# A planner's priorities replaced by a fixed table of task order, and second-layer expert weights loaded into batch tiles as these come free

## The chip, the cores and the metric

The kernel runs on one core of a Trainium2 chip. The metric is device time in microseconds (us), the median of the runs shown. The core has a matrix engine (TensorE, PE), a vector engine (VectorE, DVE), a scalar engine (ScalarE, ACT), a general engine (GpSimd, POOL) and a queue engine that here only issues transfers (SyncE, SP). POOL and ACT can issue transfers (DMAs) too. Each engine takes its instructions in the order of the program, and waits at an instruction until what it needs is there.

## The reference

For 8 batches of 3072 tokens and 256 channels the kernel computes a Fourier mixing layer, a soft mixture of experts over all tokens, and a gated feed-forward layer:

```python
X = np.fft.rfft(x, axis=1)
Yr = Xr @ w_r - Xi @ w_i + b_r
Yi = Xr @ w_i + Xi @ w_r + b_i
Yr = np.sign(Yr) * np.maximum(np.abs(Yr) - lam, 0.0)
Yi = np.sign(Yi) * np.maximum(np.abs(Yi) - lam, 0.0)
y = np.fft.irfft(Y, n=x.shape[1], axis=1)
...
logits = x @ phi
d = np.exp(logits - logits.max(0)); d /= d.sum(0) + 1e-09
slot_input = d.T @ x
h = np.maximum(slot_input[e] @ w1[e], 0.0)
slot_out[e] = h @ w2[e]
c = np.exp(logits - logits.max(1)); c /= c.sum(1) + 1e-09
x = c @ slot_out
...
g = x @ w_gate
silu = g * (1.0 / (1.0 + np.exp(-g)))
val = x @ w_val
return (silu * val @ w_out).astype(np.float32)
```

The second softmax (`d`) runs over all 24576 tokens, so no expert can start before the last batch is through.

## The kernel before

There are three parts. **The planned part** treats the eight batches. The transform of 3072 points is split into 96 x 32: `stage_a` (PE, then a transposition `turn` on DVE) makes the 96-point half from quarters of `x` (`load_x`, two buffers), `stage_c` the 32-point half for three groups of frequencies, with evacuations on ACT and DVE, `stage_b` multiplies by the mixed weights (bank `pb`), `after_b` applies the threshold (`take`, `gather`, two `relu`, and `join`, a subtraction). `stage_q` multiplies the result `yt` by `phi` (PE products that are 32 columns wide, four side by side), turns `yt` on DVE (`turn_y`) and copies it in 16 pieces to the slots' layout `yi` with DMAs (`spread`). When three groups are through, `logits` goes back to the time domain (`inv_mm` from `qt`), takes maxima and exponentials, `slots` transforms these forward again (`rot` and `cross` are its rotations, `d_mm` a product) and multiplies them by `yi` (`slot_mm`, again 32 wide; `acc` gathers over the batches), `combine` prepares the third softmax and stores it. In between, `narrow` converts the weights of the last layer, which arrive as 64-bit numbers, in 18 pieces: load, `bits` and `value` on DVE, `size` on ACT, store.

Every step is a task that names what it reads, writes and needs. `Plan` holds them; rings (`plan.ring`) say how many buffers a kind of tile has. `Plan.run` is a list scheduler: it holds a model of each engine with durations (`COST`), a rank for each task with a correction (`SHIFT`), and always emits the task that can start first. So all engines' orders come out of this one loop. A task for `POOL` or `DVE` goes where the model has it done sooner. `hold` is a filler for PE: a product of the identity that nobody reads, taken only when PE would be idle.

**The expert part** (`after_slots`) needs `acc` from all batches. `stage1` multiplies by the first-layer weights (`w1s`, 1 MB for each of 8 experts), `turn` transposes, `stage2` multiplies by the second-layer weights (`w2s`, 1 MB each), in two rounds of four experts. First-layer loads are issued by POOL from the seventh batch on. Of the second-layer loads one goes out on POOL into a `yi` buffer; the other seven are issued by SP, when the last batch's `yi` pieces are through and the pool `bpool` (the batches' tiles) is closed by `free_b`, into a new pool `w2p` in its place. After them SP loads the gate weights (`fetch_wg`, three tiles `wg`).

**The steady part** first makes the gates (`gates`, tile `pq`), then runs 576 steps `gv`, `split`, `mm_out` over all tokens; its order is written out and not the planner's.

The key of the scheduler, in `Plan.run`, is:

```python
                    start = max(free.get(eng, 0.0) + turn, can, lock if pair(t, eng) else 0.0)
                    late = self.SHY if eng == "DVE" and len(t["eng"]) > 1 else 0.0
                    key = (start + late + self.PULL * t["rank"], t["rank"], start + late + dur, i)
```

Of the kernel before, what the change touches and what calls it, by code (L numbers as in the profile page):

```python
# [176 lines left out]
SHIFT = {  # L177
    "load_f": 57.75,
    "setup_small": -9.60,
    "load_first": -50.92,  # L180
    "stage_a.mm": -37.34,
    "stage_a.turn": 178.17,
    "put": 21.58,
    "free_early": -22.55,
    "load_w": 17.51,
    "mix_w": 61.49,
    "part_w": 18.49,
    "rest_w": -44.08,
    "stage_c.mm": (-53.77, 60.00, -28.03),
    "stage_c.hi": (67.58, -4.36, -34.90),  # L190
    "stage_c.lo": (-43.26, 302.18, -37.48),
    "stage_c.one_part": (-45.81, -35.81, 101.37),
    "stage_c.add_part": (-86.88, 268.31, 3.85),
    "stage_c.sum_hi": (-10.55, -273.23, -22.13),
    "stage_c.sum_lo": (-20.53, 76.87, -19.92),
    "stage_c.last_mm": (77.17, -43.48, -22.30),
    "stage_c.last_out": (64.11, 2.06, 26.30),
    "stage_b.last_mm": (-36.93, 87.21, 10.64),
    "stage_b.last_out": (61.99, -49.29, 73.95),
    "stage_b.mm": (59.64, 39.68, 49.11),  # L200
    "after_b.take": (184.64, -139.65, -117.21),
    "after_b.gather": (160.13, -11.80, -62.89),
    "after_b.relu": (577.81, 16.03, 90.14),
    "after_b.join": (15.07, 342.92, 39.20),
    "stage_q.mm": (77.93, -329.29, -32.38),
    "stage_q.turn_y": (0.20, 193.63, -56.74),
    "stage_q.turn": (130.59, 74.27, 57.66),
    "stage_q.spread": (11.96, 122.22, 36.67),
    "logits.inv_mm": 8.02,
    "logits.sp_mm": 56.11,  # L210
    "logits.sp_out": -28.82,
    "logits.rot": 154.63,
    "logits.join": 49.80,
    "logits.turn": -29.07,
    "logits.l_mm": 8.04,
    "logits.colmax": 29.69,
    "logits.keep_l": 48.70,
    "logits.spread": 152.32,
    "logits.max_mm": -95.72,
    "logits.newmax": 11.02,  # L220
    "logits.factor": -30.34,
    "logits.bc_mm": -17.70,
    "logits.lower": 61.38,
    "logits.expo": 71.85,
    "slots.f_mm": -192.46,
    "slots.turn": 242.98,
    "slots.cross": 121.42,
    "slots.rot": -1492.94,
    "slots.join": 46.30,
    "slots.d_mm": -85.36,  # L230
    "slots.evac": -50.96,
    "slots.slot_mm": -0.37,
    "slots.gather": -37.26,
    "combine.rowmax": 980.32,
    "combine.lower": -94.57,
    "combine.expo": 30.36,
    "combine.total": 0.43,
    "combine.scale": -18.67,
    "combine.turn": 30.84,
    "combine.hi": 77.39,  # L240
    "combine.lo": 100.87,
    "combine.store": 99.47,
    "narrow.load": -15.44,
    "narrow.bits": 876.30,
    "narrow.size": -12.04,
    "narrow.value": -46.30,
    "narrow.store": -30.91,
    "load_x": 70.05,
    "narrow.part": -34.22,
    "narrow.rest": 42.69,  # L250
    "stage_q.mm'": (33.76, 59.91, 56.58),
    "stage_q.turn_y'": (15.84, 57.75, 66.51),
    "stage_q.turn'": (-73.17, -38.23, -63.13),
    "stage_q.spread'": (-79.12, -25.52, 3.84),
    "logits.inv_mm'": -43.32,
    "logits.sp_mm'": 58.71,
    "logits.sp_out'": 7.77,
    "logits.rot'": 26.85,
    "logits.join'": 98.80,
    "logits.turn'": 6.52,  # L260
    "logits.l_mm'": 27.21,
    "logits.colmax'": 31.11,
    "logits.keep_l'": 106.81,
    "logits.spread'": -3.41,
    "logits.max_mm'": -5.61,
    "logits.newmax'": 3.65,
    "logits.factor'": 8.54,
    "logits.bc_mm'": 107.77,
    "logits.lower'": -53.83,
    "logits.expo'": 10.94,  # L270
    "slots.f_mm'": 44.65,
    "slots.turn'": 29.30,
    "slots.cross'": 150.69,
    "slots.rot'": -35.92,
    "slots.join'": 40.15,
    "slots.d_mm'": 40.12,
    "slots.evac'": -10.89,
    "slots.slot_mm'": -39.73,
    "slots.gather'": -26.36,
    "combine.rowmax'": -21.56,  # L280
    "combine.lower'": -6.29,
    "combine.expo'": 33.50,
    "combine.total'": -63.42,
    "combine.scale'": -88.17,
    "combine.turn'": -137.59,
    "combine.hi'": 68.96,
    "combine.lo'": -28.54,
    "combine.store'": 69.48,
    "free_x": -87.13,
    "free_a": -92.66,  # L290
    "free_b": 58.33,
    "fetch_w1": 102.65,
    "fetch_w2": 19.16,
    "fetch_wg": 51.16,
    "hold": 519.95,
    "stage_c.mm'": 31.70,
    "stage_c.hi'": 180.69,
    "stage_c.lo'": 40.92,
    "stage_c.one_part'": -78.25,
    "stage_c.add_part'": 37.03,  # L300
    "stage_c.sum_hi'": 68.22,
    "stage_c.sum_lo'": 8.91,
    "stage_b.mm'": 107.80,
    "after_b.take'": -12.15,
    "after_b.gather'": -45.62,
    "after_b.relu'": -8.39,
    "after_b.join'": 21.85,
# [1616 lines left out]
```

## Time and profile before

| | |
|---|---|
| median of 3 runs | 1716.13 us (1716.11 to 1717.84) |
| the profiled execution | 1717.98 us |
| its span (first to last instruction) | 1716.2 us |
| mean granted clock of PE | 0.997 |
| PE busy | 1676.7 us (98%), 8176 matrix instructions |
| DVE busy | 1276.8 us (74%) |
| ACT busy | 983.0 us (57%) |
| POOL busy | 351.3 us (20%) |
| DMA | 139.95 MB, mean 82 GB/s |
| longest groups on PE | `mm_out` with `hh` 722.5 us, with `hl` 453.8 us |

The planned part ends near 600 us, the steady loop begins near 640. An engine's busy share says little here: PE is the bound nearly everywhere, and what it loses is seen in its waits and in the time that its instructions take. A matrix instruction in a row of the timeline is an entry; several entries make a product.

### The profile page before, as it was taken

The numbers are of one execution on the slowest core, as the hardware profiler recorded it, in microseconds if no ns is written. First come the engines' busy times: TensorE is split into PE (matmuls) and PEld (weight loads), VectorE is DVE, ScalarE is ACT, GpSimd is POOL, SyncE is SP. The second block draws the span as 40 slices with busy tenths as digits, with TensorE's granted clock in tenths as the row PEclk, the third lists the DMA queues.
The fourth block names the chain that finished last, engine by engine and source line by source line (L and its number), as shares of the span: only waits on it lengthen the run. The fifth ranks groups of instructions, "written<-read, shape, count | busy, mean of one in ns | idle before, by whom it ended". The sixth has DMA issues, their size and how long they took to land.

```text
span 1716.2 us, 23315 instructions
## 1 busy us (share of the span) xinstructions
PE 1676.7 (98%) x8176; PEld 1283.8 (75%) x8176; DVE 1276.8 (74%) x2156; ACT 983.0 (57%) x1830; POOL 351.3 (20%) x392
## 2 busy tenths in 40 slices
PE   7999999999999979999999999999999999999998
PEld 4677676776767638888888888888888888888886
DVE  4677878878786628777777777777777877877776
ACT  2565554655556326666655656666666655666664
POOL 1345433344444620200200100010110110110000
PEclk9999999999999999999999999999999999999999
...
GB/s 188 80 105 149 113 136 132 111 157 112 144 141 137 236 337 14 81 25 25 78 28 26 49 57 25 29 72 18 25 81 25 25 80 25 25 71 25 25 25 25
DMA packets 260421, 139.95 MB, mean 82 GB/s; under 512 B 210224, under 2 KB 244240, under 8 KB 260304
## 3 DMA queue, kind: packets, MB, share of 16 engines
...
q14 instruction: 52, 0.43, 0.1%
...
## 4 chain that ended last, share of the span: by engine, by line
PE 89%; DMA 3%; DVE 3%; ACT 2%; SPq 2%; issue 1%; POOL 0%; ACTq 0%; DVEq 0%
PE o L1804 47%; PE pb L881 10%; PE pg L1779 8%; PE pv L1780 8%; PE ac L764 6%; PE ac L786 4%; PE ch L1050 1%; PE ch L979 1%; SPq L1008 1%; PE ch L1252 1%; DMA wg<-w_scr 1%; DVE xg L808 1%; PE ch L1304 1%; DMA w2s<-in_moe_w_dram 1%; DVE sf L814 1%; DMA cvi<-in_moe_w_out_dram 1%
## 5 line engine op out<-in xcount | busy, mean ns | idle before, releaser
L1804 PE MATMUL o<-hh,wo 128*128 128x512 f32 x2304 | 722.5, 394 | 0.0
L1782 ACT ACTIVATE sg<-pg 128x512 f32<-128x512 f32 x576 | 344.9, 599 | 418.0 <-PE pg L1779 418.0
L1784 DVE TENSOR_TENSOR h<-sg,pv 128x512 f32<-128x512 f32 x576 | 393.5, 683 | 251.2 <-ACT sg L1782 248.8
L1804 PEld LDWEIGHTS o<-hh,wo 128*128 128x128 f32 x2304 | 434.3, 188 | 100.8
L1804 PE MATMUL o<-hl,wo 128*128 128x512 f32 x1152 | 453.8, 394 | 0.0
L1792 DVE TENSOR_TENSOR hl<-h,hh 128x512 fp32r<-128x512 f32 x576 | 398.0, 691 | 0.1
L1791 ACT ACTIVATE hh<-h 128x512 fp32r<-128x512 f32 x576 | 359.3, 624 | 0.2 <-DVE h L1784 0.2
L1804 PEld LDWEIGHTS o<-hl,wo 128*128 128x128 f32 x1152 | 216.1, 188 | 51.8
L1779 PE MATMUL pg<-cst,gstk 96*128 96x512 f32 x576 | 227.8, 395 | 0.0
L1780 PE MATMUL pv<-cst,gstk 96*128 96x512 f32 x576 | 226.0, 392 | 0.0
L953 POOL TENSOR_TENSOR yt<-r,yt 128x512 f32<-128x512 f32 x96 | 125.5, 1307 | 166.8 <-ACT yt L944 91.8
L881 PE MATMUL pb<-xg,wh 128*128 128x512 f32 x384 | 142.5, 452 | 2.0 <-ACT yt L934 1.6
L1780 PEld LDWEIGHTS pv<-cst,gstk 96*128 96x128 f32 x576 | 109.7, 190 | 25.1
L1779 PEld LDWEIGHTS pg<-cst,gstk 96*128 96x128 f32 x576 | 108.1, 188 | 25.7 <-DVE gstk L1765 0.8
L1840 POOL TENSOR_TENSOR e<-e,rs 96x256 f32<-96x256 f32 x28 | 22.2, 818 | 500.0 <-DVE rs L1837 500.0
L769 DVE STREAM_TRANSPOSE chan<-ac 128x512 f32<-128x512 f32 x128 | 89.3, 706 | 36.6 <-PE ac L764 33.5
L764 PE MATMUL ac<-xq,fwd 96*128 96x512 f32 x224 | 110.2, 603 | 1.7 <-DVE m L1130 1.1
L786 PEld LDWEIGHTS ac<-cm,chan 128*128 128x128 f32 x768 | 99.3, 196 | 14.0 <-issue 7.0
L786 PE MATMUL ac<-cm,chan 128*128 128x128 f32 x768 | 104.8, 285 | 0.8 <-ACT sg L823 0.8
L881 PEld LDWEIGHTS pb<-xg,wh 128*128 128x128 f32 x384 | 66.9, 189 | 34.9 <-issue 19.6
L827 POOL TENSOR_TENSOR sg<-sf,sg 128x256 fp32r<-128x256 f32 x96 | 69.9, 741 | 88.9 <-ACT sg L823 72.7
L814 DVE TENSOR_TENSOR sf<-ac,sf 128x256 f32<-128x256 f32 x96 | 40.4, 421 | 49.9 <-ACT sf L811 21.2
...
## 6 DMA issues: line engine op xcount, KB each, us to landing
out_dram<-ob SPq DMA_DIRECT2D x190, 128.0 KB, 2.8
...
w2s<-in_moe_w_dram SPq DMA_DIRECT2D x7, 1024.0 KB, 12.9
x<-in_x_dram SPq DMA_DIRECT2D x4, 768.0 KB, 11.6
...
```

The lines of the kernel that those rows point to most:

```text
L764: nc.tensor.matmul(out=pt, lhsT=fwd[:, 8 - 8 * dh:136 - 8 * dh], rhs=T[kq][:, :, d1:d1 + 16], start=True, stop=True)
L769: nc.vector.transpose(out=chan[:, 12 * dh:12 * dh + 16, d0:d0 + 16, :].rearrange("p j d i -> p d j i"), in_=T[ka].rearrange("p n d -> p d n"),
L786: nc.tensor.matmul(out=pt[:, :, q:q + 2, i // 2, :], lhsT=chan[:, 16 * dh + j // 2, :, j % 2], rhs=cm[:, j, :].rearrange("p (c h k) -> p c ...
L881: nc.tensor.matmul(out=pt, lhsT=w[:, dh, m, es], rhs=xx, start=m != 1 and dh == 0 and n == 0, stop=dh == 1 and n == 2, skip_group_check=True,)
L953: e.tensor_sub(out=part(), in0=quarters(T[kr]), in1=part())
L1779: nc.tensor.matmul(out=pg, lhsT=gstk[:, 0, f * 128:(f + 1) * 128], rhs=rhs, start=True, stop=True)
L1780: nc.tensor.matmul(out=pv, lhsT=gstk[:, 1, f * 128:(f + 1) * 128], rhs=rhs, start=True, stop=True)
L1782: nc.scalar.activation(out=sg, in_=pg, func=AF.Silu)
L1784: nc.vector.tensor_mul(out=h, in0=sg, in1=pv)
L1791: nc.scalar.activation(out=hh, in_=h, func=AF.Copy)
L1792: nc.vector.tensor_sub(out=hl, in0=h, in1=hh.bitcast(F32))
L1804: nc.tensor.matmul(out=po_t[0][k], lhsT=w[:, f % 4, k * 128:(k + 1) * 128], rhs=a, start=(f == 0 and m == 0), stop=(f == NF - 1 and m == 2 ...
```

## The change

The tables `SHIFT`, `COST` and `PAIR` and the scheduler go. In their place stands `ORDER`, a table of task numbers; a negative number means that the task goes to the second of its two engines (DVE). `Plan.run` only emits the tasks in this order, and stops if one comes before what it needs. Each task keeps its work. Besides the order:

- The second-layer loads all go out on POOL, into tiles of the batches: experts 0 to 3 into the four buffers of `xg`, 4 into that of `sg`, 5 into that of the mixed weights (`wh` and `wl` are now one tile `whl`), 6 into the conversion tile `cv`, 7 into a `yi` buffer. `free_b` and `w2p` go; `bpool` is closed after `stage2`. `fold` is loaded at the start.
- The first three first-layer loads wait for the second half of the last conversion. The gate weights no longer wait for the second-layer loads.
- The conversion's input and its two outputs are one tile `cv` with one buffer, so a load waits for the store before it.
- In the last two groups `yi` is copied in four parts by SP and POOL (before: in the last group only).

```diff
+ORDER = [
+    2, 1, 0, 3, 4, 5, 40, 30, 50, 312, 48, 49, 6, 8, 7, 9, 10, 12, 11, 13,
...
-    def run(self):
...
+    def run(self, order, spare=()):
         rings = {name: [] for name in self.bufs}
...
+        kept = {i if i >= 0 else ~i for i in order}
+        done = set()
+        for i in order:
+            t = self.tasks[i if i >= 0 else ~i]
+            need = set(t["deps"])
+            for name, home in t["new"]:
+                row, n = rings[name], self.bufs[name]
+                if len(row) >= n:
+                    need |= row[-n]["users"] & kept
+                row.append(home)
+            if not need <= done:
+                raise RuntimeError("a task comes before what it needs")
+            t["fn"](t["eng"][i < 0]) if isinstance(t["eng"], tuple) else t["fn"]()
+            done.add(t["i"])
...
-    def load_w2(pool, e):
-        tag, bufs = ("w2", E - 1) if e < E - 1 else ("yi", 4)
-        w2_t[e] = pool.tile([128, 8, 256], F32, tag=tag, name="w2s", bufs=bufs)
-        dma = nc.sync if e < E - 1 else nc.gpsimd
-        dma.dma_start(
+    def load_w2(pool, tag, bufs, e):
+        t = pool.tile([128, 12 if tag == "whl" else 8, 256], F32, tag=tag, name="w2s", bufs=bufs)
+        w2_t[e] = t[:, 0:8]
+        nc.gpsimd.dma_start(
...
             def load():
-                t = sb(chp, ki, [128, 512, 2], "cvi", dt=I32)
+                cv = sb(chp, ki, [128, 2048], "cv", dt=I32)
+                t = T[*ki, "i"] = cv[:, 0:1024].rearrange("p (c t) -> p c t", t=2)
+                T[*ki, "a"], T[*ki, "p"] = cv[:, 1024:1536], cv[:, 1536:2048]
                 nc.sync.dma_start(out=t.rearrange("p (u c) t -> p u (c t)", u=src.shape[1]), in_=src)
...
-        def free_b():
-            close_pool("bpool")
-            pools["w2p"] = p = open_pool("w2p", "right")
-            fold["t"] = p.tile([128, 128], F32, name="fold")
-            nc.sync.dma_start(out=fold["t"], in_=csmall[:, FOLD:FOLD + 128])
...
         for e in range(E):
...
             add(
+                "POOL", fetch_w1(e), r=["w1a" if e < 3 else "w1b"], w=[("w1", e)], after=[("yi", last, 0, 0) if e > 2 else ("cv", len(jobs) - 1)],
             )
+        w2_at = {e: (bpool, f"xg{e % 2}", 2) for e in range(4)}
+        w2_at |= {4: (bpool, "sg", 1), 5: (bpool, "whl", 1), 6: (chp, "cv", 1), 7: (None, "yi", 4)}
+        pbs = [("pb", last, 2, eh, d, 0) for eh in range(2) for d in range(2)]
+        xgs = [("xg", last, 2, 0, 0, 0)]
+        for e, new, behind in (
+            (6, "cv", [("ws", len(jobs) - 1)]), (7, "yi", [("yi", last, 0, 0)]), (0, "xg", xgs), (1, "", xgs + ["w20"]),
+            (2, "xg", xgs + ["w21"]), (3, "", xgs + ["w22"]), (4, "sg", [("sg", last, 2, 0, 0, 0)]), (5, "", pbs),
+        ):
+            add("POOL", fetch_w2(e), w=[f"w2{e}"], new=(new, f"w2{e}") if new else None, after=behind)
         for t in (0, 1):
             add(
...
+                "SP", fetch_wg(t), w=[("wg", t)], new=("yt", ("wg", t)), after=[("ws", i) for i, (_, d) in enumerate(jobs) if len(d) == 1] + [("yt", last, 2, 0, 1)],
             )
...
-        plan.run()
+        plan.run(ORDER, range(spare, len(plan.tasks)))
...
-        close_pool("mps", "w2p")
+        close_pool("mps", "bpool")
```

How the table moves instructions is seen at three places. The first is on DVE, in batch 6, around the last `turn` that makes `qt` ready for the inverse transform; before, the last conversion (`cvi` to `cv`) stands ahead of it:

```order
L1409 TENSOR_SCALAR cv_4745<-cvi_4621 128x512
L1410 SCALAR_TENSOR_TENSOR cv_4745<-cvi_4621,cv_4745 128x512
L1411 SCALAR_TENSOR_TENSOR cv_4745<-cvi_4621,cv_4745 128x512
L1428 SCALAR_TENSOR_TENSOR cv_4746<-cvi_4621,cv_4745 128x256 x2
L995 STREAM_TRANSPOSE yt_4583<-yt_4583 128x1024
L990 STREAM_TRANSPOSE qt_4439<-ch_4642 128x2x128
L937 TENSOR_TENSOR yt_4730<-pb_4725,yt_4730 128x4x128
```

After, at the same place (L808 is `qt`, L1207 to L1209 the conversion):

```order
L808 STREAM_TRANSPOSE qt_4262<-ch_4615 128x2x128
L813 STREAM_TRANSPOSE yt_4459<-yt_4459 128x1024 x2
L720 TENSOR_REDUCE yz_100<-ch_4629 128x2
L721 TENSOR_TENSOR yz_100<-yz_100,bdif_101 128x2
L755 TENSOR_TENSOR yt_4661<-pb_4580,yt_4661 128x4x128
L757 COPY yt_4661<-yz_100 128x1
L1207 TENSOR_SCALAR cv_4639<-cv_4639 128x512
L1208 SCALAR_TENSOR_TENSOR cv_4639<-cv_4639 128x512
L1209 SCALAR_TENSOR_TENSOR cv_4639<-cv_4639 128x512
```

The conversion has moved from ahead of `qt` to five rows behind it.

The second is on PE, where batch 6's slot products meet the last `stage_q` (`ch<-yt,phis`), ahead of batch 7's inverse transform (`ch<-qt`); before, with fillers (`pb<-ident`):

```order
L1304 MATMUL ch<-yi,p_5151 32x256 x20
L979 MATMUL ch<-yt,phis 32x256 x4
L1619 MATMUL pb<-ident 128x128
L979 MATMUL ch<-yt,phis 32x256 x4
L1050 MATMUL ch<-qt,csm 128x192 x8
L1088 MATMUL ch<-qt,csm 64x32 x2
L1619 MATMUL pb<-ident 128x128 x8
```

After (the first half of the last `stage_q` stands just ahead of the slot products):

```order
L1103 MATMUL ch<-yi,p_5102 32x256 x12
L797 MATMUL ch<-yt,phis 32x256 x4
L1103 MATMUL ch<-yi,p_5102 32x256 x8
L865 MATMUL ch<-qt,csm 128x192 x4
L903 MATMUL ch<-qt,csm 64x32 x2
L865 MATMUL ch<-qt,csm 128x192 x4
L1387 MATMUL pb<-ident 128x128 x4
```

Slot products now stand around the second half of `stage_q`, and no filler is left between them.

The third is POOL's queue at the end of the planned part: joins (L953), the last `yi` pieces, the rotations `p<-vt` of batch 7, and the loads. Before (the other seven second-layer loads are SP's, behind its `yi` pieces):

```order
L1036 TENSOR_TENSOR p_5060<-vt,csm 128x384 x2
L953 TENSOR_TENSOR yt<-r,yt 128x4x128
L605 DMA w1s<-in_moe_w_dram 128x2x1024 x5
L953 TENSOR_TENSOR yt<-r,yt 128x4x128 x2
L1342 TENSOR_TENSOR ls<-ls,rm 96x1024
L953 TENSOR_TENSOR yt<-r,yt 128x4x128
L611 DMA w2s<-in_moe_w_dram 128x2x1024
L953 TENSOR_TENSOR yt<-r,yt 128x4x128
L1008 DMA yi<-yt 32x2x256 x8
L1036 TENSOR_TENSOR p_5342<-vt,csm 128x384 x2
L1342 TENSOR_TENSOR ls<-ls,rm 96x1024
L1642 MEMSET h1t 128x2048
```

After, from the last join to the last second-layer load:

```order
L771 TENSOR_TENSOR yt<-r,yt 128x4x128
L826 DMA yi<-yt 32x2x256 x2
L1140 TENSOR_TENSOR ls<-ls,rm 96x1024
L826 DMA yi<-yt 32x2x256 x6
L427 DMA w1s<-in_moe_w_dram 128x2x1024
L826 DMA yi<-yt 32x2x256 x2
L427 DMA w1s<-in_moe_w_dram 128x2x1024 x2
L826 DMA yi<-yt 32x2x256 x6
L851 TENSOR_TENSOR p_5281<-vt,csm 128x384
L432 DMA w2s<-in_moe_w_dram 128x2x1024 x4
L1140 TENSOR_TENSOR ls<-ls,rm 96x1024
L432 DMA w2s<-in_moe_w_dram 128x2x1024
```

Three first-layer loads now stand among `yi` pieces, one rotation of two is left, and five second-layer loads stand behind it; the other three second-layer loads stand ahead of the join.

## Rows read from the trace of the kernel before

**Rows 1.** Busy time in stretches: us, each engine (instructions), PEclk, DMA share, GB/s.
```profile
60.00:500.00 440.00, 435.33 (x2486) 304.50 (x2485) 353.32 (x621) 251.37 (x498) 187.29 (x174) 1.00 0.62 129
526.00:536.00 10.00, 6.75 (x33) 6.25 (x25) 7.81 (x16) 6.36 (x13) 5.82 (x6) 0.70 0.19 46
600.80:628.20 27.40, 21.05 (x214) 9.49 (x214) 3.23 (x35) 2.88 (x6) 6.40 (x11) 0.94 1.11 370
...
641.00:1716.20 1075.20, 1068.79 (x4603) 866.83 (x4601) 819.31 (x1317) 651.69 (x1179) 82.87 (x125) 1.00 0.20 40
```
**Rows 2.** PE's waits to 640 us: us in total, times, longest.
```profile
PE po L1692 <- DMA w2s<-in_moe_w_dram: 5.7, 3, 2.6
...
PE pq L1754 <- DMA wg<-w_scr: 2.4, 3, 1.8
...
PE ac L764 <- ACT sg L823: 2.1, 1, 2.1
```
**Rows 3.** PE's timeline, 500 to 562 us: start, us, instruction [idle before].
```profile
525.75 0.64 PE L979 MATMUL ch<-yt,phis 128*32 128x256 f32 x8
526.32 1.21 PE L786 MATMUL ac<-cm,chan 128*128 128x128 f32 x8
530.77 5.49 PE L1050 MATMUL ch<-qt,csm 128*128 128x192 f32 x16 [3.25 <-DVE qt L990]
...
543.84 0.40 PE L881 MATMUL pb<-xg,wl 128*128 128x512 f32 x1
544.17 1.07 PE L979 MATMUL ch<-yt,phis 128*32 128x256 f32 x16
545.17 0.73 PE L881 MATMUL pb<-xg,wh 128*128 128x512 f32 x2
545.74 0.40 PE L881 MATMUL pb<-xg,wl 128*128 128x512 f32 x1
545.98 1.10 PE L786 MATMUL ac<-cm,chan 128*128 128x128 f32 x8
```
**Rows 4.** PE's timeline, 555 to 642 us.
```profile
574.85 0.49 PE L1619 MATMUL pb<-ident 128*128 128x128 f32 x2
...
576.80 2.87 PE L1050 MATMUL ch<-qt,csm 128*128 128x192 f32 x16 [0.57 <-DVE qt L990]
...
593.13 1.54 PE L1252 MATMUL ch<-vpad,csm 128*128 128x192 f32 x8 [0.52 <-DVE vpad L1241]
...
608.32 0.63 PE L1692 MATMUL po<-w2s,h1t 128*32 128x256 f32 x6
...
614.83 1.93 PE L1692 MATMUL po<-w2s,h1t 128*32 128x256 f32 x32
...
622.40 5.23 PE L1692 MATMUL po<-w2s,h1t 128*32 128x256 f32 x60 [2.62 <-DMA w2s<-in_moe_w_dram]
```
**Rows 5.** DVE's timeline, 514 to 536 us.
```profile
526.48 0.43 DVE L1409 TENSOR_SCALAR cv<-cvi 128x512 int32<-128x512 int32 x1 [3.93 <-DMA cvi<-in_moe_w_out_dram]
...
530.31 0.41 DVE L990 STREAM_TRANSPOSE qt<-ch 128x256 f32<-128x256 f32 x1
```
**Rows 6.** The conversion's loads (tile `cvi`), issue to landing.
```profile
DMA to landing us min/median/max: 3.3/5.0/11.7
```
**Rows 7.** The second-layer loads (tile `w2s`), issue to landing.
```profile
DMA to landing us min/median/max: 5.1/12.9/22.9
```
**Rows 8.** POOL's timeline, 560 to 640 us: the rotations of batch 7.
```profile
590.14 2.63 POOL L1036 TENSOR_TENSOR p<-vt,csm 128x384 f32<-128x384 f32 x2 [3.03 <-DVE vt L1216]
```
**Rows 9.** The first-layer loads (tile `w1s`), issue to landing.
```profile
DMA to landing us min/median/max: 5.3/8.7/15.5
```
**Rows 10.** POOL's groups, 60 to 500 us: busy us, mean ns, idle before.
```profile
L953 POOL TENSOR_TENSOR yt<-r,yt 128x512 f32<-128x512 f32 x75 | 98.1, 1309 | 139.9 <-ACT yt L944 66.7 <-DMA yi<-yt 34.4 <-ACT r L944 25.5
```
**Rows 11.** DVE's groups, 60 to 500 us.
```profile
L808 DVE TENSOR_TENSOR xg<-ac,xg 128x512 fp32r<-128x512 f32 x76 | 51.8, 686 | 11.6 <-ACT xg L805 11.2
```
**Rows 12.** SP's own waits, 60 to 540 us.
```profile
SPq L1443 <- DVE cv L1428: 31.2, 4, 8.2
```

More of the change, by code (lines that the diff above doesn't have):

```diff
@@ L174 @@
 FOLD = FWD + SMW
[L177 to L307, printed above, removed]
-    "slots.f_mm''": 0.86,
-    "slots.turn''": -111.76,
-    "slots.cross''": -36.41,
-    "slots.rot''": 22.29,
-    "slots.join''": 6.65,
-    "slots.d_mm''": 45.97,
-    "slots.evac''": -23.32,
-    "slots.slot_mm''": 36.71,
-    "slots.gather''": -13.41,
-}
@@ L386 @@
-PAIR = {
-    "mix_w",
-    "rest_w",
-    "stage_c.sum_lo",
-    "after_b.join",
-    "logits.join",
-    "logits.spread",
-    "logits.newmax",
-    "slots.cross",
-    "slots.rot",
-    "slots.join",
-    "narrow.bits",
-    "narrow.value",
-    "narrow.rest",
-}
-class Plan:
-    LAG, OUT, IN = 0.04, 0.2, 0.155
-    TILED, TURN = {"stage_q.mm", "slots.slot_mm"}, (0.22, 0.095)
-    HAND, SET, SEEN = 0.65, 0.9, 0.65
-    SHY = 0.18
-    PULL = 0.001
-    def __init__(self, shift):
+ORDER = [
[121 rows of a table added]
+]
@@ L782, in mm @@
                 pt = bank(kc, [128, 2, 4, 2, 32], "ac")
+                sb(bpool, ks, [128, 4, 64], "sf", 2)
+                if hb == 0 and dh == 0:
+                    for s in range(2):
+                        sb(bpool, (*kx, s), [128, 2, 2, 512], f"xg{s}", 2, F32R)
                 for i in range(4):
@@ L1448, in store @@
                         nc.sync.dma_start(out=o[:, u].rearrange("p (h x) -> p h x", h=2), in_=t[:, u])
-            add("SP", 0.06, rank, load, w=[ki], new=("cvi", ki), bus=1.46, after=[("ac", "a", b, 15)])
-            add("DVE", 2.0, rank + 0.3, bits, w=[ki, ka], new=("cv", ka))
-            add("ACT", 0.5, rank + 0.3, size, w=[ki])
-            add("DVE", 0.65, rank + 0.3, value, w=[ki, ka])
+            add("SP", load, w=[ki], new=("cv", ki), after=[("ac", "a", b, 15)])
+            add("DVE", bits, w=[ki])
+            add("ACT", size, w=[ki])
+            add("DVE", value, w=[ki])
             if len(dst) == 2:
-                add("ACT", 0.5, rank + 0.3, part, w=[ka])
-                add({"POOL": 1.23, "DVE": 0.6}, 0, rank + 0.3, rest, w=[ka])
-            add("SP", 0.12, rank + 0.4, store, r=[ka], w=[("ws", i)], bus=0.74 * len(dst), dmas=len(dst) ** 2)
+                add("ACT", part, w=[ki])
+                add(("POOL", "DVE"), rest, w=[ki])
+            add("SP", store, r=[ki], w=[("ws", i)])
         jobs = []
```

416 lines of the change are left out of this document (108 added, 308 removed), and 122 rows, old and new, of tables (ORDER, add).

## The prediction

> **What bounds the kernel now.** I read the stretches first, then the waits of TensorE (PE), then its timeline around each long wait, then what the waited-for engine did. From 641 us to the end PE is busy for 1068.79 of 1075.20 us [rows 1]; that part (the loop `gv`, `split`, `mm_out`) is outside the planner and its code is unchanged, so I take it as unchanged. Everything the change can move lies in the first 641 us. There PE is nearly full as well: from 60 to 500 us it is busy for 435.33 of 440, so only 4.7 us of visible idle is to be had there [rows 1]. The losses sit in a few places: in the list of waits up to 640 us the largest that the table can reach are the second-layer weights (5.7 us in three waits), the gate weights (2.4 in three) and one wait of 2.1 at the start [rows 2].
>
> **The late conversion tile.** From 526 to 536 us PE is busy for 6.75 of 10 us, and the mean granted clock is 0.70: part of it ran at the lower of its two levels, 1.2 of 2.4 GHz [rows 1]. PE stands still for 3.25 us before the inverse transform of batch 6, waiting for DVE's `qt`; those 16 entries then take 5.49 us [rows 3], while the same 16 of batch 7 take 2.87 us at full clock [rows 4]. The wait and the slow run cost 3.25 + 2.62 = 5.9 us. The cause is one engine further on: DVE had reached the conversion `narrow.bits` and stood 3.93 us for its DMA, with `qt`, which PE needed, queued behind it until 530.31 [rows 5]. That DMA is the slowest of its eighteen: the maximum is 11.7 us, the median 5.0 [rows 6], and three first-layer loads had just gone out on POOL. The change acts on both: it lets first-layer weights start loading only when the last conversion has its second half, and in the new order `qt` stands ahead of the conversion on DVE. What is late next is `narrow` itself, whose result nobody needs before the transition. I count all 5.9; bounds 3.3 (the clock drops elsewhere) and 5.9.
>
> **The expert weights.** Before, seven of the eight second-layer loads are issued by SP after the last `yi` pieces and land in 5.1 to 22.9 us, median 12.9 [rows 7]. PE waits 5.7 us for them [rows 2], and after the last wait the clock is at the lower level for a while (0.94 is the mean of the stretch [rows 1]): 60 entries take 5.23 us where 32 at full clock take 1.93 [rows 4], so 60 would take 3.6 and 1.6 is lost. After the change all eight go out on POOL: experts 0, 1 and 5 before the last `yi` pieces, experts 2, 7, 6 and 3 behind POOL's one rotation of batch 7, and 4 last. That rotation starts at 590.14 before [rows 8]; one of them takes about 1.3 us, so the four go out from about 591.5. Loads of this size from POOL (the first-layer weights) landed in 5.3 to 15.5 us, median 8.7 [rows 9]. With the median, expert 3, the last of the four, is there by 604, before `stage2`, which starts at 608.32 before [rows 4] and some 2 us sooner after the change; with the maximum it is not. Expert 4, issued some 3 us later, is needed only in the second round. I go by the median and count 5.7 + 1.6 = 7.3; bounds 0 (all land as late as before) and 7.3.
>
> The seven loads were also ahead of the gate weights in SP's queue. Without them I count 1.8 of the 2.4 us that PE waits for gate weights [rows 2]; the rest is handed to ScalarE (ACT), which must finish the first gates anyway. Bounds 0 and 2.4. `fold` moves to the start: one more DMA of 64 KB in a queue that PE does not wait for, at nothing; if uncovered, its issue of about half a microsecond.
>
> One rule speaks against sending these loads from POOL. The Trainium skill, "SBUF — State Buffer", section "SBUF: two separate sides", says that a DMA issued from GpSimd can starve while VectorE holds the port pair they share, and advises the SP or ACT queue instead. By it the loads would gain nothing. The trace does not bear it out for this kernel, since the loads from POOL landed sooner by the median, 8.7 against 12.9 us [rows 7, 9].
>
> **The end of the planned part.** Between the first half of the last `stage_q` and the inverse transform of batch 7 PE runs a filler, waits, runs the second half of `stage_q`, and waits again, 0.57 us: of the 1.95 us from 574.85 to 576.80 [rows 4] only that second half, 0.57 us as below, is needed work. In the new order slot products that are already possible stand around the second half of `stage_q`. I count 1.0 of the 1.4. Later POOL does both rotations of batch 7, 2.63 us [rows 8], and PE waits at 593.13 for the sums behind them [rows 4]. After the change DVE does the second one itself. The second sum still bounds the second half, so I count 0.8. Together 1.8; bounds 0 and 2.4.
>
> **Switches of TensorE between full and 32-wide products.** A run of one `stage_q` call takes 0.57 us to the next start (525.75 to 526.32), a run of two takes 1.00 (544.17 to 545.17): the second call costs 0.43, so leaving a run costs 0.14. Entering costs 0.09: after one product of `pb` the next start comes after 0.33 (543.84 to 544.17) where it comes after 0.24 at a full-width successor (545.74 to 545.98) [rows 3]. In the orders of PE I count 43 such runs before and 26 after, because halves of `stage_q` now stand together or beside slot products. 17 x 0.23 = 3.9 us. Bounds 1 (where the switch was hidden in a wait) and 3.9.
>
> **The start and the rest.** Of the 2.1 us wait near 27 us [rows 2] I count 1.0: fifteen instead of fourteen `stage_a` products now precede the first `stage_c`, but the mixing of weights still stands on DVE ahead of the evacuation. Bounds 0 and 2.1. Against this, 22 joins (128x512) and 22 `sum_lo` go from POOL to DVE, plus three smaller tasks. A join took 1.31 us on POOL [rows 10]; on DVE the nearest row, a subtraction of the same size, takes 0.69 [rows 11], and I price a `sum_lo`, half as large, at 0.4: some 24 us more on an engine that was busy for 353 of 440 us [rows 1]. That raises it from about 80% to 85%; the work lies beside PE, so I count nothing, and price a miss below. The order in the middle gets irregular; I take its net as zero, with 4.7 us as the most that it can win of visible idle.
>
> **Sum.** 5.9 + 7.3 + 1.8 + 1.8 + 3.9 + 1.0 = 21.7 us. The profiled execution took 1717.98 us (span 1716.2, with 1.8 around it), 1.85 above the median of the runs. So 1717.98 - 21.7 = 1696.3 in its terms, and 1694.4 in the median's; I say 1694.5.
>
> **Rivals.**
> First, the late loads stay late: POOL's in-order queue, with `yi` pieces, first-layer loads and the rotation ahead of the second-layer loads, pushes them back, or the rule above holds. For it: five of the eight still go out after 590 us. Against: the POOL landings. Then the 7.3 stay and the time is 1694.4 + 7.3 = 1702.
> Second, DVE becomes late for PE: the 47 moved tasks stand ahead of evacuations. If each delays PE by 0.2 us, 9 us come back: 1704. For it: 353 of 440 us busy. Against: a join is done 0.6 us sooner on DVE, and PE's waits in the middle are now few.
> Third, on the other side: slower. `narrow` now keeps its input and both outputs in one tile, so the load of piece i+1 waits on SP until the store of piece i has landed, and the store waits on SP for DVE, with the loads of `x` and the `yi` pieces queued behind. Already before, four stores waited 31.2 us on SP for the conversion, up to 8.2 each [rows 12], and PE had no wait for `x` after the start among its larger waits [rows 2], so the two buffers of `x` covered that. If the cover is gone, each of 18 pieces stalls PE: it decides from 21.7 + 3.4 = 25 us, 1.4 us a piece; at 1.8 a piece the time is 1694.4 + 32 = 1727.
> Fourth, the new order does nothing net: small waits all over the irregular middle, about 2.5 us a batch, use up the gain: 1715.
>
> **Chances.** A measurement here tells a change from none at about 0.2%, 3.4 us. My forecast 0.66, with its own range 1688 to 1700; first rival 0.12 (1702), second 0.10 (1704), third 0.06 (1727), fourth 0.06 (1715). The bottom is all upper bounds and the idle of the middle: 21.7 + 0.6 + 0.6 + 1.1 + 4.7 = 28.7 us, 1687. The top is the second rival with some spread, 1706; left out are the third and fourth rivals and the tails of the others, some 0.16. Faster by over 0.2%: 0.66 + 0.12 + 0.10 = 0.88; within 0.2%: the fourth, 0.06; slower: the third, 0.06.
>
> **What would show it.** The first step is right if PE has no wait over 1 us for `qt` of batch 6 and the clock shows no half-speed stretch near 530 us. The second: no wait of PE for second-layer weights, and from the first product with `acc` to the steady loop about 9 us less than before. The third: gate weights landed before `gates(2)`. The fifth: some 0.6 us less a batch where nothing waits. It would be wrong if PE's waits between 60 and 500 us grew above 10 us, if PE waited for `x`, or if a half-clock stretch appeared inside the first 600 us.

## The result

The changed kernel takes 1693.64 us (median of 4 runs, 1692.41 to 1695.34) against 1716.43 before (1716.11 to 1717.84): a ratio of 0.9866, with a 95% interval of 0.9849 to 0.9883. The forecast was 1694.5. Its profiled execution has a span of 1691.6 us, against 1716.2. So the time came out. Most terms of the sum did not, and their errors cancelled.

The profile is first read in stretches, with the columns of [rows 1]. The first row runs from the point where PE has done 41 us of work to the point where it has done 490, counting each kind of product at its mean time in the steady batches of before (the numbers of entries, x2560 here and x2568 before, show how nearly the work is the same). The second holds the inverse transform of batch 6, the next two are short stretches at a lower mean granted clock, the fifth runs from `pst` to the steady loop, and the sixth is the loop.

```profile
56.44:497.22 440.78, 438.23 (x2560) 313.99 (x2559) 371.33 (x656) 253.43 (x506) 164.96 (x153) 1.00 0.64 131
510.00:520.00 10.00, 10.00 (x55) 8.78 (x54) 9.18 (x21) 9.03 (x18) 5.71 (x5) 1.00 0.49 108
572.00:576.00 4.00, 3.05 (x16) 2.72 (x17) 3.32 (x7) 0.49 (x1) 1.16 (x2) 0.78 0.97 232
596.00:600.00 4.00, 4.00 (x38) 1.55 (x30) 0.00 (x0) 0.00 (x0) 0.00 (x0) 0.73 0.67 259
583.66:616.96 33.30, 28.36 (x251) 12.57 (x252) 7.99 (x43) 9.66 (x17) 11.83 (x18) 0.95 1.18 326
616.96:1691.60 1074.64, 1068.30 (x4601) 866.39 (x4599) 818.39 (x1318) 651.21 (x1179) 83.39 (x125) 1.00 0.21 40
```

Before, the first and the fifth of these stretches were:

```profile
59.38:510.83 451.45, 446.78 (x2568) 310.92 (x2566) 361.82 (x633) 255.20 (x503) 192.61 (x178) 1.00 0.62 128
600.77:641.46 40.69, 31.56 (x251) 13.46 (x252) 8.24 (x43) 8.70 (x16) 9.69 (x16) 0.96 1.22 348
```

The steady batches are 10.67 us shorter, and only 2.12 of that is idle time (4.67 to 2.55): PE is busy 8.55 us less for the same products. The expert part, with the gates, is 7.4 us shorter. The steady loop is unchanged. PE's waits to 640 us after the change:

```profile
PE po L1460 <- DMA w2s<-in_moe_w_dram: 3.2, 1, 3.2
PE ch L1055 <- DVE vpad L1044: 2.8, 1, 2.8
PE ch L1103 <- DMA w2s<-in_moe_w_dram: 1.1, 1, 1.1
PE ac L586 <- DVE xg L631: 1.0, 1, 1.0
```

The waits for gate weights [rows 2] and for `qt` [rows 3] are gone; of the 5.7 us for second-layer weights 3.2 are left. Two waits at the end of the planned part are new, of 2.8 and 1.1 us. PE's timeline shows both, and ahead of them the inverse transform of batch 6 (514 us), which now runs at full clock without a wait [rows 3]:

```profile
514.09 1.46 PE L865 MATMUL ch<-qt,csm 128*128 128x192 f32 x8
516.32 1.47 PE L865 MATMUL ch<-qt,csm 128*128 128x192 f32 x8
...
554.24 1.57 PE L865 MATMUL ch<-qt,csm 128*128 128x192 f32 x8
...
572.95 1.64 PE L1055 MATMUL ch<-vpad,csm 128*128 128x192 f32 x8 [2.80 <-DVE vpad L1044]
...
580.62 2.37 PE L1103 MATMUL ch<-yi,p 128*32 128x256 f32 x40 [1.13 <-DMA w2s<-in_moe_w_dram]
583.66 0.63 PE L1420 MATMUL pst<-fold,acc 128*128 128x32 f32 x4 [0.68 <-DVE acc L1122]
...
595.05 3.17 PE L1460 MATMUL po<-w2s,h1t 128*32 128x256 f32 x25 [3.21 <-DMA w2s<-in_moe_w_dram]
...
616.96 0.64 PE L1572 MATMUL o<-hh,wo 128*128 128x512 f32 x2
```

The 2.80 us at 572.95 end with POOL's rotation, which DVE needed for `vpad` and which stood behind a stop in POOL's queue, as DVE's timeline and POOL's show:

```profile
572.44 0.63 DVE L1044 TENSOR_TENSOR vpad<-vpad,p 128x192 f32<-128x192 f32 x2 [3.41 <-POOL p L851]
```

```profile
562.67 1.63 POOL L826 DMA_DIRECT2D yi<-yt  x3
569.80 1.60 POOL L826 DMA_DIRECT2D yi<-yt  x3 [5.50 <-DMA w1s<-in_moe_w_dram]
571.41 1.00 POOL L851 TENSOR_TENSOR p<-vt,csm 128x384 f32<-128x384 f32 x1
...
579.28 2.14 POOL L432 DMA_DIRECT2D w2s<-in_moe_w_dram  x3 [4.18 <-DMA w1s<-in_moe_w_dram]
```

POOL did not issue the next transfer until a first-layer load had landed. This wait stands in the program. In the trace POOL's transfers use eight semaphores (the counters that tell of a landing) in turn, so that each transfer stands behind the landing of the one eight issues ahead of it, which had the same semaphore. The piece at 569.80 waits for the load issued at 559.43, which landed at 569.51. In none of the fourteen traces does a transfer of POOL start before the one eight ahead of it has landed. The kernel before had such a stop too, at POOL's last `yi` piece:

```profile
586.57 0.54 POOL L1008 DMA_DIRECT2D yi<-yt  x1 [4.26 <-DMA w2s<-in_moe_w_dram]
```

The 1.13 us at 580.62 carry the name of a `w2s` load that uses a semaphore of the pieces again; by the landings it was the piece issued at 569.80, there at 580.44, that ended them.

Cut at the inverse transform of batch 7 (576.80 before [rows 4], 554.24 after), the gain of the two profiles is 22.6 us ahead of it, 1.9 from there to the steady loop (64.7 against 62.7 us), and 0.1 in the loop.

### The profile page after: what moved, and what is told of

The parts are those of the page before. It is cut to its first block, busy times and chain, and to the rows that moved or that the text cites. A ratio compares the mean times of both kernels' runs of the same rounds, so it can differ in the third digit from the quotient of the medians.

```text
span 1691.6 us, 23302 instructions
## 1 busy us (share of the span) xinstructions
PE 1662.7 (98%) x8178; PEld 1284.8 (76%) x8178; DVE 1296.0 (77%) x2203; ACT 980.7 (58%) x1830; POOL 312.5 (18%) x360
## 4 chain that ended last, share of the span: by engine, by line
PE 94%; DMA 3%; DVE 1%; POOL 1%; ACT 0%; issue 0%; SPq 0%; DVEq 0%; ACTq 0%
PE o L1572 47%; PE pb L700 11%; PE pg L1547 8%; PE pv L1548 8%; PE ac L586 7%; PE ac L612 5%; PE ch L797 1%; PE ch L865 1%; PE ch L1055 1%; DMA w1s<-in_moe_w_dram 1%; PE ch L1103 1%; DMA w2s<-in_moe_w_dram 1%; PE ch L925 1%; PE ch L1011 1%; PE po L1460 1%; DMA xq<-in_x_dram 0%
## 5 line engine op out<-in xcount | busy, mean ns | idle before, releaser
L700 PE MATMUL pb<-xg,whl 128*128 128x512 f32 x576 | 179.3, 441 | 0.0
L700 PEld LDWEIGHTS pb<-xg,whl 128*128 128x128 f32 x576 | 105.3, 189 | 46.5 <-issue 25.1
L771 POOL TENSOR_TENSOR yt<-r,yt 128x512 f32<-128x512 f32 x74 | 96.6, 1305 | 153.5 <-ACT yt L762 103.2
L591 DVE STREAM_TRANSPOSE chan<-ac 128x512 f32<-128x512 f32 x128 | 89.8, 708 | 34.1 <-PE ac L586 29.8
L1608 POOL TENSOR_TENSOR e<-e,rs 96x256 f32<-96x256 f32 x28 | 22.6, 834 | 498.8 <-DVE rs L1605 498.8
L700 PE MATMUL pb<-sg,whl 128*128 128x512 f32 x288 | 86.7, 425 | 0.0
L634 ACT ACTIVATE sf<-ac 128x256 f32<-128x256 f32 x96 | 36.5, 381 | 78.5 <-PE ac L612 74.4
## 6 DMA issues: line engine op xcount, KB each, us to landing
w2s<-in_moe_w_dram POOLq DMA_DIRECT2D x8, 1024.0 KB, 10.9
```

The costliest lines, as they stand in the source:

```text
L591: nc.vector.transpose(out=chan[:, 12 * dh:12 * dh + 16, d0:d0 + 16, :].rearrange("p j d i -> p d j i"), in_=T[ka].rearrange("p n d -> p d n"),
L700: nc.tensor.matmul(out=pt, lhsT=w[:, dh, m, es], rhs=xx, start=m != 1 and dh == 0 and n == 0, stop=dh == 1 and n == 2, skip_group_check=True,)
L771: e.tensor_sub(out=part(), in0=quarters(T[kr]), in1=part())
```

## The experiments

Theory: the two parts of the change each carry their terms of the sum, the order 12.6 us and the early weights 9.1. Rival: the order carries all, and the transfers at the end are bound by what the DMA engines can move. Each kernel was timed beside the kernel before. In the changed table 2325 is the first rotation of batch 7, 2357 to 2364 are the first-layer loads of experts 0 to 7, 2365 to 2372 the second-layer loads of experts 6, 7 and 0 to 5.

**The late conversion.** Two kernels keep the code of before and its own task order, written out as a table (line numbers 66 higher). The first moves the three first-layer loads (2350 to 2352 there) behind the last conversion's subtraction (2345):

```diff
...
-    1988, 2344, 2164, 2142, 2345, 2172, 1989, 1990, 2143, 2137, 1991, 2175, 2139, 2346, 2173, 2169, 2170, 2176, 1997,
+    1988, 2344, 2164, 2142, 2345, 2350, 2351, 2352, 2172, 1989, 1990, 2143, 2137, 1991, 2175, 2139, 2346, 2173, 2169, 2170, 2176, 1997,
```

> The kernel before, its own task order written out as a table, with one move: the first three first-layer loads stand on POOL behind the last conversion's subtraction instead of ahead of it. Theory A, that these loads make the last conversion's DMA slow (11.7 us against a median of 5.0): it lands in about 5 us, DVE's 3.93 us wait for it goes, PE's 3.25 us wait for `qt` and the lower clock behind it go, and the time falls by 5 to 6 us, to 1710 or 1711. Theory B, that only the conversion's place ahead of `qt` on DVE counts and its DMA is late anyway: within 1.5 us of 1716.

Measured: 1713.57 against 1716.09, ratio 0.9986 (0.9978 to 0.9995). The conversion's load, the only one between 500 and 545 us, and PE's timeline:

```profile
DMA to landing us min/median/max: 4.2/4.2/4.2
```

```profile
528.06 2.87 PE L1116 MATMUL ch<-qt,csm 128*128 128x192 f32 x16 [0.63 <-DVE qt L1056]
...
532.73 0.50 PE L947 MATMUL pb<-sg,wh 128*128 128x512 f32 x1 [1.57 <-POOL sg L893]
```

The load takes 4.2 us instead of 11.7, the wait falls from 3.25 to 0.63 and the 16 entries take 2.87 instead of 5.49 [rows 3]. Theory A holds for the mechanism; the time lies between the two forecasts. POOL gives 1.57 us back, since `sum_lo` now stands behind the three loads that it issues; in the profile `pst` comes 4.3 us sooner, in the medians 2.5 are left.

The second leaves the loads and moves the conversion's steps (2341 to 2345) behind `qt` (1989):

```diff
...
-    1988, 2344, 2164, 2142, 2345, 2172, 1989, 1990, 2143, 2137, 1991, 2175, 2139, 2346, 2173, 2169, 2170, 2176, 1997,
+    1988, 2164, 2142, 2172, 1989, 1990, 2143, 2341, 2342, 2343, 2344, 2345, 2137, 1991, 2175, 2139, 2346, 2173, 2169, 2170, 2176, 1997,
```

> The kernel before, its own task order written out as a table, with one move: the last conversion's steps stand behind `qt` of batch 6 and the two tasks that follow it; the first-layer loads stay where they are. Theory B, that the place on DVE is what counts: PE's wait for `qt` and the lower clock go though the DMA stays slow, 5 to 6 us less, 1710 or 1711. Rival, that the wait only moves to what stands behind the conversion now (`rot` of batch 6, evacuations of batch 7): at most 2 us less, 1714 to 1716.

Measured: 1718.3, ratio 1.001 (1.0001 to 1.0019). PE's timeline, then POOL's:

```profile
527.90 2.87 PE L1116 MATMUL ch<-qt,csm 128*128 128x192 f32 x16 [0.63 <-DVE qt L1056]
533.62 0.50 PE L947 MATMUL pb<-sg,wh 128*128 128x512 f32 x1 [2.85 <-ACT sg L889]
535.25 0.51 PE L947 MATMUL pb<-sg,wh 128*128 128x512 f32 x1 [1.12 <-POOL sg L893]
```

```profile
532.00 1.27 POOL L1504 TENSOR_TENSOR cv<-cv 128x512 f32<-128x512 f32 x1 [5.11 <-ACT cv L1497]
```

The transfer still takes 11.3 us. `qt` is in time, but ACT's and POOL's parts of the same late conversion now stand ahead of `sg`, and PE waits 2.85 and 1.12 us for that. The rival's mechanism holds, at a time 2.3 us above its range: the late transfer was the cause, and the conversion's place on DVE only chose who waited.

**Placement without the order.** All edits of the change, but with the tasks in the order and on the engines of before:

```diff
 ORDER = [
-    2, 1, 0, 3, 4, 5, 40, 30, 50, 312, 48, 49, 6, 8, 7, 9, 10, 12, 11, 13,
...
```

> All edits of the change but the table's order: the tasks go out in the order and on the engines of the kernel before, a task that is not possible there (a load into the single conversion tile) as soon as it is; the second-layer loads stand on POOL where their tiles come free. If placement carries the gain: PE's waits for second-layer and gate weights (5.7 and 2.4 us, and 1.6 for the clock) and the stop at 526 to 536 us (5.9, since first-layer loads go out behind the last conversion) go, 9 to 15 us less than 1716, 1701 to 1707. If the order carries it: 1712 to 1717, with the conversions on a single tile perhaps more.

Measured: 1746.3, ratio 1.0173 (1.0159 to 1.0187). PE's waits and POOL's timeline (line numbers 3 lower than in the changed kernel):

```profile
PE ch L794 <- POOL yt L768: 21.7, 2, 21.2
PE pb L697 <- POOL sg L647: 17.2, 1, 17.2
```

```profile
549.46 0.74 POOL L429 DMA_DIRECT2D w2s<-in_moe_w_dram  x1 [14.94 <-DMA w_scr<-cv]
...
601.80 0.54 POOL L823 DMA_DIRECT2D yi<-yt  x1 [3.65 <-DMA w2s<-in_moe_w_dram]
605.70 0.54 POOL L823 DMA_DIRECT2D yi<-yt  x1 [3.36 <-DMA w2s<-in_moe_w_dram]
609.08 0.54 POOL L823 DMA_DIRECT2D yi<-yt  x1 [2.85 <-DMA w2s<-in_moe_w_dram]
```

Two stops make 38.4 us: the load into `cv` waits on POOL 14.94 us for the conversion's store, with `sum_lo` behind it, and later each `yi` piece waits for the load eight issues ahead of it, with the last join behind them. Neither forecast held. Where the loads stood on POOL was this kernel's own choice, so it shows only that the placement needs an order made for it.

**The order without the placement.** The changed kernel, with seven second-layer loads on SP again (line numbers at most 2 off):

```diff
+        def free_b():
+            close_pool("bpool")
+            pools["w2p"] = open_pool("w2p", "right")
...
+        add("SP", free_b, w=["w2p"], after=[("joined", last, 2, eh, co) for eh in range(2) for co in range(2)])
+        add("POOL", fetch_w2(E - 1), w=["w27"], new=("yi", "w27"), after=[("yi", last, 0, 0)])
+        for e in range(E - 1):
+            add("SP", fetch_w2(e), r=["w2p"], w=[f"w2{e}"])
```

> The changed kernel with its table, but seven second-layer loads go out on SP behind its last `yi` pieces into a pool of their own, as in the kernel before. If placement is worth what the expert part gained (7.4 us from `pst` to the steady loop): that part is 7 us longer, and POOL's hold-up at the end of the planned part stays since it comes from first-layer loads: about 1700. If it is worth nothing, because the DMA engines are full from 540 us on whoever issues: 1692 to 1695.

Measured: 1694.21, ratio 0.9876 (0.9862 to 0.989), the changed kernel's own time. PE's waits, and SP's timeline:

```profile
PE ch L1104 <- DMA yi<-yt: 4.3, 1, 4.3
PE ch L1056 <- DVE vpad L1045: 3.1, 1, 3.1
```

```profile
566.13 18.42 SPq L433 DMA_DIRECT2D w2s<-in_moe_w_dram  x7
```

The expert part got shorter, not longer: in the new order SP is through with its `yi` pieces some 30 us sooner than before, and its loads go out from 566 us. In return the slot products wait for pieces. The first forecast falls; the second, that who issues does not matter, holds.

**What the end is bound by.** Three kernels move work at the end of the changed table. `rot_dve` gives POOL's last rotation to DVE:

```diff
-    2393, 2394, 2395, 2396, 2397, 2323, 2317, 2328, 2324, 2326, 2329, 2325, 2369, 2327, 2366, 2331, 2398, 2399, 2400, 2401,
+    2393, 2394, 2395, 2396, 2397, 2323, 2317, 2328, 2324, 2326, 2329, -2326, 2369, 2327, 2366, 2331, 2398, 2399, 2400, 2401,
```

> The changed kernel, with the one rotation of batch 7 that is left on POOL (`cross`, first half) given to DVE. Theory A, that the end of the planned part is late because this rotation stands in POOL's queue behind loads: PE's wait of 2.80 us for `vpad` before the first product `d` of batch 7 goes, the lower clock behind it (0.78 from 572 to 576 us) goes too, and the time falls by 3 to 4 us from 1693.6, to about 1690. Theory B, that the `yi` pieces, which POOL issues just as late (569.8 to 571.4 us), set the end: PE's wait before the slot products grows from 1.1 us to about 4, and the time stays within 1 us of 1693.6.

`w1_behind` puts three first-layer loads behind that rotation:

```diff
...
+    2393, 2394, 2395, 2396, 2397, 2323, 2317, 2328, 2324, 2326, 2329, 2325, 2360, 2361, 2362, 2369, 2327, 2366, 2331, 2398, 2399, 2400, 2401,
```

> The changed kernel, with the first-layer loads of experts 3, 4 and 5, which stand among the last `yi` pieces on POOL, moved behind POOL's last rotation. Theory A, that these three loads hold up POOL (5.5 us before its last three pieces): the pieces go out by about 566 us, the rotation starts near 568 instead of 571.4, PE's two waits of 2.8 and 1.1 us go, and the time falls by 4 to 5 us, to 1689 or 1690; the loads then go out near 570 and at the median of 9.0 us land by 580, before `stage1` wants expert 3. Theory B, that POOL waits for loads sent earlier: the hold-up stays, only the loads come later, `stage1` or `stage2` waits 3 to 5 us more, and the time is 1696 to 1698.

`need_order` sorts the loads by need, and gives the rotation to DVE too:

```diff
...
+    2353, 2173, 2147, 2176, 2144, 1995, 2358, 2354, 2148, 2145, -2172, 2186, 2150, 1996, 2146, 2179, 2177, 2174, 2357, 2359, 2149,
...
+    2314, 2310, 2385, 2386, 2387, 2388, 2315, 2223, 2316, 2313, 2389, 2390, 2391, 2318, 2293, 2361, 2362, 2363, 2364, 2371, 2372, 2365, 2366, 2319, 2321, 2320, 2322, 2392,
```

> The changed kernel, with the weight loads put in the order in which the expert part needs them: on POOL the first-layer loads of experts 0 to 3 and the second-layer loads of 0 to 3 go out before the last `yi` pieces, the eight loads of experts 4 to 7 behind the last piece; the rotation left on POOL goes to DVE. Theory A, that the waits at the end come from the wrong loads being first: pieces go out by 566 us, no wait for `vpad` (2.8) or before the slot products (1.1), none for second-layer weights in the first round (3.2), and the clock stays high: 8 to 9 us less than 1693.6, about 1685. Theory B, that the DMA engines are full from 540 us on and what one place wins another loses, as in the two runs that moved loads: 1691 to 1695.

A fourth leaves out four second-layer loads, and a fifth is the changed kernel as it is:

```diff
     def load_w2(pool, tag, bufs, e):
+        if e > 3:
+            w2_t[e] = w2_t[0]
+            return
```

> The changed kernel without four of its weight loads: the second-layer weights of experts 4 to 7 are not loaded, their products read expert 0's tile instead (so this leaves out 4 of the 16 MB of expert weights, and the second half of the expert sum is another one). Theory A, that from 540 to 600 us the amount to be moved is the bound: PE's wait of 3.2 us for second-layer weights goes and the loads finish some 10 us sooner; the time falls by at least 4 us, to 1689 or less. Theory B, that the order of POOL's queue alone makes the waits: the rotation is still held up by first-layer loads (PE's waits of 2.8 and 1.1 us stay), the load of expert 3 goes out when it did, and the time stays within 2 us of 1693.6.

> The changed kernel as it is, once more, as the measure for the runs that differ from it by 1 to 3 us. Every theory: 1692.4 to 1695.3, its earlier runs.

Measured, with the stretches from PE's timelines (starts of batch 7's inverse transform, of `pst`, and of the steady loop):

| kernel | median us | ratio to before | inverse transform to `pst` | `pst` to loop | both |
|---|---|---|---|---|---|
| before | 1716.43 | 1 | 24.0 | 40.7 | 64.7 |
| changed | 1693.64 | 0.9866 (0.9849 to 0.9883) | 29.4 | 33.3 | 62.7 |
| `after_again` | 1692.43 | 0.9863 (0.9846 to 0.9879) | 30.0 | 34.6 | 64.6 |
| `rot_dve` | 1691.56 | 0.9862 (0.9845 to 0.9878) | 30.5 | 31.2 | 61.7 |
| `w1_behind` | 1694.93 | 0.9883 (0.9868 to 0.9898) | 23.8 | 41.6 | 65.4 |
| `need_order` | 1692.43 | 0.9859 (0.9845 to 0.9874) | 23.9 | 37.2 | 61.1 |
| `new_old_w2` | 1694.21 | 0.9876 (0.9862 to 0.989) | 34.4 | 29.8 | 64.2 |
| `half_w2` | 1689.23 | 0.9847 (0.9832 to 0.9862) | 28.8 | 27.9 | 56.8 |

The first stretch can be had at 24 us, as before, by clearing POOL's queue (`w1_behind`, `need_order`); each time the second grows. What clearing does is seen in the pieces that POOL issues from 562 to 564 us, in the changed kernel and in `w1_behind`:

```profile
DMA to landing us min/median/max: 16.3/16.5/16.7
```

```profile
DMA to landing us min/median/max: 2.8/2.8/3.0
```

PE's waits in `rot_dve`:

```profile
PE ch L1103 <- DMA yi<-yt: 4.6, 1, 4.6
```

in `w1_behind`:

```profile
PE po L1460 <- DMA w2s<-in_moe_w_dram: 9.4, 2, 8.4
```

in `need_order`, with its stretches:

```profile
PE po L1460 <- DMA w2s<-in_moe_w_dram: 5.6, 2, 4.6
```

```profile
560.00:570.00 10.00, 9.56 (x60) 7.27 (x59) 6.87 (x15) 2.49 (x5) 10.00 (x17) 1.00 0.91 276
570.00:580.00 10.00, 9.22 (x104) 7.39 (x102) 4.46 (x11) 2.04 (x3) 4.17 (x3) 1.00 1.02 398
580.00:590.00 10.00, 9.88 (x105) 3.65 (x104) 1.77 (x19) 1.79 (x3) 3.13 (x5) 1.00 1.03 403
```

and in `half_w2` (line numbers 3 higher):

```profile
PE ch L1058 <- DVE vpad L1047: 2.1, 1, 2.1
PE ch L1106 <- DMA yi<-yt: 1.2, 1, 1.2
```

Each redistribution moved the wait to another transfer, while the DMA engines were busy at 0.84 to 1.05 in the stretches of 10 us from 560 to 590 us. With a quarter less weight the second stretch went from 33.3 to 27.9 us, and the waits of the first stayed: theory A of that run holds for the expert part, theory B for the planned part, and 1689.23 lies between their forecasts. In `rot_dve` the trace shows what theory B said, a longer wait for pieces, and 1691.56 is too near both forecasts to choose by; `w1_behind` was right on the planned part and wrong on the rest; `need_order` came out as theory B. None of the three reorderings beats the changed kernel by more than its own runs differ; two executions of that kernel differ by 1.9 us in the last column as well. `half_w2` takes four transfers out of POOL's queue along with their bytes and does not part the two. That `new_old_w2`, with seven loads on another queue, and `need_order`, with all in another order, stay at 64.2 and 61.1 us speaks for the bytes.

**Joins on POOL again.** 44 signs of the table, of which two:

```diff
-    72, 100, 79, 80, 118, 76, -82, 87, 77, 121, 119, 101, 122, 299, 74, 125, 88, 102, 82, 128,
-    126, 129, 85, 123, 83, 95, 130, 124, 89, 96, 120, 90, 107, -132, 91, 132, 127, 98, -93, 139,
...
```

> The changed kernel with its table, but the 22 joins and 22 `sum_lo` that it gives to DVE run on POOL again, as before. The prediction's theory, that this work lies beside PE on either engine: 1693 to 1697 (a join takes 1.3 us on POOL and 0.7 on DVE, so a chain behind it may get later). Rival, that DVE is late for PE because of the moved work (the second rival of the prediction): about 9 us less, 1685.

Measured: 1697.34, ratio 0.9896 (0.9881 to 0.9911). The steady batches, for the same work as above:

```profile
56.88:498.39 441.51, 438.50 (x2560) 313.75 (x2558) 359.78 (x632) 253.41 (x506) 188.66 (x177) 1.00 0.64 131
```

That is 0.7 us more than in the changed kernel: there the work lies beside PE on either engine, and the rival's 1685 falls. From the end of this stretch to batch 7's inverse transform it does not lie beside PE, here and in the changed kernel:

```profile
498.39:559.66 61.27, 58.03 (x385) 43.00 (x384) 47.77 (x79) 38.18 (x76) 38.82 (x41) 1.00 0.65 209
```

```profile
497.22:554.24 57.02, 57.01 (x386) 43.27 (x384) 48.46 (x92) 38.46 (x76) 25.50 (x27) 1.00 0.66 215
```

That is 4.2 us more, of which 3.2 are idle time of PE; 3.9 of them come back between the inverse transform and the loop (58.8 against 62.7 us). The profiled execution was the fastest of the four, 1694.9 us, so these stretches make 1.5 us; where the other runs lose the rest of the 3.7 is not shown.

**Switches to 32-wide products.** 18 second calls of `stage_q` moved one PE task on, of which one (114):

```diff
...
-    189, 162, 190, 115, 160, 304, 161, 163, 113, 146, 164, 191, 117, 147, 185, 305, 192, 313, 193, 151,
+    189, 162, 114, 190, 115, 160, 304, 161, 163, 113, 146, 164, 191, 117, 147, 185, 305, 192, 313, 193, 151,
```

> The changed kernel, with 18 of its pairs of `stage_q` calls on PE taken apart: the second call of each stands one full-width task later, so that PE has 18 more runs of 32-wide products. If a run costs 0.23 us in switches, as the prediction has it: 18 x 0.23 = 4.1 us more, 1697.8. If switches cost nothing, or stand in time that PE would lose anyway: within 1 us of 1693.6.

Measured: 1701.38, ratio 0.9921 (0.9906 to 0.9936), 7.7 us more. For the same work:

```profile
56.69:503.77 447.08, 443.06 (x2559) 312.58 (x2558) 371.46 (x657) 253.52 (x506) 165.04 (x153) 1.00 0.63 129
```

In this stretch there are 34 runs of such products here and 20 in the changed kernel: 14 more cost 6.30 us, 4.83 busy and 1.47 idle, so 0.35 busy and 0.45 in all for each. Both forecasts were too small, the first by nearly half.

The reverse, 15 pairs brought together in the order of before, of which one (112 and 113):

```diff
...
-    311, 301, 159, 315, 160, 302, 314, 163, 316, 317, 161, 164, 185, 174, 165, 192, 186, 166, 114, 318, 193, 319, 115,
+    311, 301, 159, 315, 160, 302, 314, 163, 316, 317, 161, 164, 185, 174, 165, 192, 186, 166, 112, 114, 113, 318, 193, 319, 115,
```

> The kernel before, its own task order written out as a table, with the first `stage_q` call of 15 groups moved on PE to stand just ahead of the second, so that PE has 28 runs of 32-wide products instead of 43. At the prediction's 0.23 us a run: 3.5 us less than 1716, 1712.5. At the 0.40 us that 18 split pairs cost in the changed kernel: 6 us less, 1710. Rival, that a call moved back by up to 19 tasks holds `yt` too long and stalls PE: 1716 or more, with a new wait of PE in the profile.

Measured: 1734.27, ratio 1.0104 (1.0087 to 1.012). PE's largest wait after the start:

```profile
PE ch L1116 <- DVE qt L1056: 10.8, 8, 4.0
```

The rival held: stalls buried the effect, and this run says nothing of a switch's price.

## Why the prediction was right

The time was right, its parts were not. Measured in the two profiles against what the prediction set down:

| stretch | predicted | measured |
|---|---|---|
| late conversion tile | 5.9 | 5.8 (3.25, and 5.49 - 2.93) |
| the rest up to batch 7's inverse transform: switches 3.9, start 1.0, filler 1.0 | 5.9 | 16.8 (22.6 - 5.8) |
| from there to the steady loop: weights 7.3, gates 1.8, last rotation 0.8 | 9.9 | 1.9 |
| steady loop | 0 | 0.1 |
| sum | 21.7 | 24.6 |

In the medians the gain is 22.8 us. The end fell 8.0 us short of its forecast and the stretch ahead of it won 10.9 more than its own, so that the time came out is luck.

**The late conversion tile** was right in place, size and cause: `old_w1_late` shows the loads as the cause of the slow transfer, and `old_conv_behind` that the place on DVE alone gives nothing.

**The switches** had the right mechanism and too small a size. The 0.23 us was read at a run's entry and exit alone; `split_q` shows 0.35 us of busy time. At that price the 14 runs fewer in the steady batches (20 against 34 before) make 4.8 of the 8.55 us by which PE was busy less.

**The step that failed in the middle** is "I take its net as zero, with 4.7 us as the most that it can win of visible idle". The visible idle gave 2.1. The bound was wrong because a busy PE is not PE at its best: what an order costs in switches is counted as busy. Some 3.7 of the 8.55 us and the 2.9 us gained ahead of the steady batches (forecast for the start: 1.0) were not taken apart by any run and stay open. Between the steady batches and batch 7's inverse transform 3.1 us were gained besides the late tile; `joins_pool` loses 4.2 there, so the joins on DVE may have won them.

**The step that failed at the end** is "I go by the median and count 5.7 + 1.6 = 7.3". The expert part and the gates did gain 7.4 us, against 9.1 predicted, but not by the placement: `new_old_w2` has the time without it. And 5.4 of it was paid just before, where 24.0 us became 29.4 in place of the forecast gain. The first rival's queue on POOL was there, in a place the prediction had not looked at: it weighed what POOL's queue does to the loads, not what the loads do to POOL's queue, where a transfer stops until the one eight ahead of it has landed. The 8.0 us missing at the end are near the 7.3 that this rival took off. The load that the step hung on, expert 3's, was issued at 580.71 and landed at 594.91, after 14.2 us in place of the median of 8.7, and PE waited 3.21 us for it. Taking landing times of before for those of after assumed transfers that leave each other alone; they do not, since the same weights in another order or on another queue gave nearly the same end.

The Trainium skill, "DMA: Bandwidth & Descriptors", section "Issuing engines are not separate DMA queues", says that transfers from any engine end on the same 16 DMA engines and interleave there. These runs agree: 1694.21 us with seven loads on SP, 1693.64 with all on POOL.

**The second rival**, an overloaded DVE, does not show: with the joins back on POOL the steady batches are 0.7 us longer, not shorter. **The third**, SP blocked by the single conversion tile, does not show in PE's waits. Of the signs that would make the forecast right the second came only in part, 7.4 us of 9 and a wait left for second-layer weights. Of those that would make it wrong one came true: the granted clock fell within the first 600 us (0.78 from 572 to 576, 0.73 from 596 to 600), behind the waits at 572.95 and 595.05.
